# A linear-attention and MLP-mixer kernel: values and kv laid out with 80 columns to a head

## The chip, the cores and the metric

The kernel runs on one core of a Trainium2 chip. The metric is the device time of one execution in microseconds. Three runs of the kernel before took 282.59, 282.40 and 282.09 us, a median of 282.4 us. A profile is one execution with the hardware profiler on; its engines are TensorE (PE in the profile, with PEld for its weight loads), VectorE (DVE), ScalarE (ACT), GpSimd (POOL) and SyncE (SP), which only issues DMAs here.

## The reference

Eight batches of eight heads, 576 positions, 64 numbers to a head. First an attention without softmax:

```python
r = np.maximum(x, 0.0);  phi = concat([r * cos_w, r * sin_w], axis=-1)   # 64 -> 128 features, for q and k
kv  = np.einsum('bhsf,bhsd->bhfd', k_p, v)
z   = np.sum(k_p, axis=2)
num = np.einsum('bhsf,bhfd->bhsd', q_p, kv)
den = np.einsum('bhsf,bhf->bhs', q_p, z)[..., None] + 1e-06
x   = num / den                    # then [batch, 576, 8 heads * 64 = 512]
```

Then an MLP-mixer on x: `u = x + tokens`, where tokens is a two-layer ReLU network along the 576 positions (576 to 256 to 576), and `out = u + channels`, a two-layer ReLU network along the 512 columns (512 to 1536 to 512). Inputs and output are float32; the matmuls are in bf16.

## The kernel before, in words

**Tiling.** A batch's 576 positions are cut into four chunks of 128 positions and a tail of 64. Each of the 128 partitions holds four positions (chunk `ci` is the ci-th position of every partition). The tail's heads 0 to 3 lie in the lower 64 partitions and heads 4 to 7 in the upper 64, so the tail is a fifth chunk with half the heads (`ci == R`, R = 4).

**The front of a batch** (class `Front`) is the attention and the token network. DVE makes the features of k and q in bf16 (`feature`, L193). `values` (L201 on ACT, L203 on DVE) casts v into a tile `v_aug` whose heads are 65 columns apart: 64 values and a column of ones, which was set once ahead of everything (L121) and gives z as the 65th column of kv. There are two such tiles, for even and odd batches. `kv` (L213) multiplies, for each head, the 128 features of a chunk (stationary) with the 65 columns of `v_aug` (moving) and adds up over the chunks in a PSUM tile of two banks, four heads to a bank. `kv_out` (L226 on ACT, in batch 0 one half at L224 on DVE) copies each bank into a bf16 tile, `kv_sb0` and `kv_sb1`, four heads of 65 columns each. `num` (L252, tail L259) multiplies the transposed features of q (stationary, `qpT`) with a head's 65 columns of `kv_sb` (moving) into another two banks. DVE adds 1e-6 to every 65th column (L265), takes the reciprocal (L266) and multiplies the 64 others with it into `x_sb` (L267). `tok1` (L280, L284) and `tok2` (L308, L312) are the token network, L315 adds x. SP transposes u by DMA (L336) into `uT`.

**The back of a batch** (class `Channel`) is the channel network: `c_main` (L418) and `c_tail` (L428) for the twelve tiles of the 1536 hidden columns with a ReLU on ACT (L422, L433), then `o_step` (L444, tail L448), the residual on DVE (L454) and the output DMAs on SP.

**The order** is written out by hand; the tile framework adds only the waits. Batch 0 has its front alone (`first_front`), with filler matmuls of zeros (`busy`, L163) where TensorE would stand idle; `num` puts one such filler into the unused columns of its first PSUM bank (`fill=1`, L247). After that the steps of a batch's `Channel` are interleaved with the pieces of the next batch's `Front` (`pieces`): a table says behind which step each piece is issued, so in the steady batches a chunk of kv or num is eight short matmuls between the long ones of the channel network. The first chunk of num comes one step behind `kv_out`. Each engine takes its instructions in that order.

**Loads.** q, k and v of batch b+2 are loaded by SP while batch b runs (`load_batch`), each tensor by one DMA with runs of 1024 bytes and two with runs of 256 bytes for the tail. In the steady batches SP's queue holds, in this order, five DMA transposes of q's features (L241), the nine loads, outputs, the two transposes of u (L336) and more outputs.

**Tiles in SBUF** lie one behind the other in the order of the pools and of their first use: constants (`v_aug0`, `v_aug1`, then the weights and zeros), then the q, k and v tiles, features, u and `uT`, `qpT`, `kv_sb0`, `kv_sb1`, then `x_sb`, `B1`, `h1T`, `u_bf` and the small ones.

The functions that the change touches, and what calls them:

Of the kernel before, what the change touches and what calls it, by code (L numbers as in the profile page):

```python
# [10 lines left out]
BF16 = mybir.dt.bfloat16  # L11
# [5 lines left out]
def kernel(  # L17
# [15 lines left out]
    nc = tc.nc  # L33

    B, H, S, D = q.shape
# [4 lines left out]
    P = 128  # L40
    R = S // P
    SM = R * P
    ST = S - SM
    NSC = R + 1
# [2 lines left out]
    NCH = D_ch // P  # L47
    HH = H // 2
    D1 = D + 1
    DH = Dm // 2  # L50
    assert S_tok == S and Dm2 == Dm and F == P and 2 * ST == P and H == 2 * HH

# [3 lines left out]
    def half(g):  # L56
        return slice(g * ST, (g + 1) * ST)


    const = ctx.enter_context(tc.tile_pool(name="const", bufs=1))  # L60
# [3 lines left out]
    once = ctx.enter_context(tc.tile_pool(name="once", bufs=1))  # L64
# [52 lines left out]

    v_augs = []
    for i in range(2):
        va = const.tile([P, NSC, H, D1], BF16, name=f"v_aug{i}")  # L120
        nc.vector.memset(va[:, :, :, D:D1], 1.0)  # L121
        v_augs.append(va)

# [37 lines left out]
    def busy(dst, times):  # L161
        for _i in range(times):
            nc.tensor.matmul(dst, ident, zeros[:, 0:dst.shape[-1]], start=True, stop=True)  # L163
# [7 lines left out]
    class Front:  # L171
        def __init__(self, b, res):
            self.qt, self.vt, self.kt = io_tiles[b]
            self.va = v_augs[b % 2]
            self.res = res
            self.kp, self.qp = {}, {}

            self.qpT = once.tile([P, R * H + HH, P], BF16, name="qpT")
            self.kv_sb = [once.tile([P, HH, D1], BF16, name=f"kv_sb{g}") for g in range(2)]
            self.x = once.tile([P, NSC, Dm], BF16, name="x_sb")  # L180

        def feature(self, which, ci, j, heads=(0, H), on_act=False):
# [22 lines left out]
        def kv(self, ci):  # L205
            if ci == 0:
                self.kv_ps = ps_at.tile([P, 2, 512], F32, name="kv_ps", tag="at")
            if ci < R:
                each = [(g, j, slice(0, P), g * HH + j) for g in range(2) for j in range(HH)]
            else:  # L210
                each = [(g, j, half(g), j) for j in range(HH) for g in range(2)]
            for g, j, rows, i in each:
                nc.tensor.matmul(self.kv_ps[:, g, j * D1:(j + 1) * D1],  # L213
                                 self.kp[ci][rows, i, :, :].rearrange("p a b -> p (a b)"),
                                 self.va[rows, ci, i, :],
                                 start=(ci == 0 and j == 0),
                                 stop=(ci == NSC - 1 and j == HH - 1),
                                 skip_group_check=True)

        def kv_out(self, split=False):  # L220
            for g in range(2):
                dst = self.kv_sb[g].rearrange("p j d -> p (j d)")
                if split and g == 1:
                    nc.vector.tensor_copy(dst, self.kv_ps[:, g, 0:HH * D1])  # L224
                else:
                    nc.scalar.copy(dst, self.kv_ps[:, g, 0:HH * D1])  # L226

        def q_trans(self, ci, heads=(0, H)):
            lo, hi = heads if ci < R else (0, HH)
# [14 lines left out]
        def num(self, ci, fill=0):  # L244
            num_ps = ps_at.tile([P, 2, 512], F32, name="num_ps", tag="at")
            if fill:
                busy(num_ps[:, 0, HH * D1:512], 1)  # L247
            den = small.tile([P, 2, HH, 1], F32, name="den")
            if ci < R:
                for h in range(H):  # L250
                    g, j = divmod(h, HH)
                    nc.tensor.matmul(num_ps[:, g, j * D1:(j + 1) * D1],  # L252
                                     self.qpT[:, ci * H + h, :], self.kv_sb[g][:, j, :],
                                     start=True, stop=True)
                n = 2
            else:
                for j in range(HH):
                    for g in range(2):
                        nc.tensor.matmul(num_ps[half(g), 0, j * D1:(j + 1) * D1],  # L259
                                         self.qpT[:, R * H + j, half(g)], self.kv_sb[g][:, j, :],  # L260
                                         start=True, stop=True)
                n = 1
            nv = num_ps[:, 0:n, 0:HH * D1].rearrange("p g (j d) -> p g j d", d=D1)
            den = den[:, 0:n]
            nc.vector.tensor_scalar_add(den, nv[:, :, :, D:D1], 1e-6)  # L265
            nc.vector.reciprocal(den, den)  # L266
            nc.vector.tensor_mul(  # L267
                self.x[:, ci, 0:n * DH].rearrange("p (g j d) -> p g j d", g=n, j=HH),
                nv[:, :, :, 0:D], den.to_broadcast([P, n, HH, D]))

        def tok1(self, mi, chunks):
# [6 lines left out]
            for ci in chunks:  # L278
# [3 lines left out]
                else:  # L282
                    for g in range(2):
                        nc.tensor.matmul(self.b1_ps[mi][:, g * DH:(g + 1) * DH],  # L284
                                         w_tail1[:, g, cols], self.x[:, R, 0:DH],
                                         start=False, stop=False, skip_group_check=True)
# [7 lines left out]
        def tok2(self, ci, pool=None):  # L294
# [8 lines left out]
            else:  # L303
                u_ps = pool.tile([P, Dm], F32, name="u_ps", tag="at")
            n = Dm if ci < R else DH
            for ki in range(NT):
# [4 lines left out]
                for g in range(2):  # L311
                    nc.tensor.matmul(u_ps[half(g), 0:DH], w_tok2[:, ki, SM:S],  # L312
                                     self.B1[:, ki, g * DH:(g + 1) * DH],
                                     start=(ki == 0), stop=(ki == NT - 1))
# [271 lines left out]
```

## Time and profile before

| | |
|---|---|
| median of three runs | 282.4 us |
| the profiled execution | 281.66 us |
| its span | 279.9 us |
| TensorE, DVE, ACT, GpSimd busy | 266.1, 161.1, 123.1, 9.7 us |
| moved by DMA | 52.51 MB |

The busy time of TensorE counts a matmul from its start to its modelled end. Matmuls are pipelined, so one of 65 columns shows about 193 ns while the next one starts some 30 ns behind it; only the starts tell what one costs. In a group's line, the name in front of the arrow is the tile written and those behind it are read; the shape is partitions by elements; the count stands behind an x; then come the group's busy time in us, the mean of one in ns, and the idle time of its engine just ahead of such instructions with what ended it. Lines in order of time begin with the start and the length in us and merge neighbours of one kind, with their count.

### The profile page before, as it was taken

The numbers are of one execution on the slowest core, as the hardware profiler recorded it, in microseconds if no ns is written. First come the engines' busy times: TensorE is split into PE (matmuls) and PEld (weight loads), VectorE is DVE, ScalarE is ACT, GpSimd is POOL, SyncE is SP. The second block draws the span as 40 slices with busy tenths as digits, with TensorE's granted clock in tenths as the row PEclk, the third lists the DMA queues.
The fourth block names the chain that finished last, engine by engine and source line by source line (L and its number), as shares of the span: only waits on it lengthen the run. The fifth ranks groups of instructions, "written<-read, shape, count | busy, mean of one in ns | idle before, by whom it ended". The sixth has DMA issues, their size and how long they took to land.

```text
span 279.9 us, 5799 instructions
## 1 busy us (share of the span) xinstructions
PE 266.1 (95%) x2345; PEld 143.8 (51%) x2370; DVE 161.1 (58%) x395; ACT 123.1 (44%) x237; POOL 9.7 (3%) x20
## 2 busy tenths in 40 slices
PE   5987899999999999999999999999999999999993
PEld 2653666545554455545554455545554455545542
DVE  2877781857576494557566485558467576540021
ACT  2642569048723186036624185137614274225500
POOL 3240020000000000000000000000000000000000
PEclk9999999999999999999999999999999999999999
DMA  6999999921779945992789648994789653161012
GB/s 170 347 192 256 340 181 267 358 89 40 163 215 341 178 112 128 341 294 101 161 257 328 177 103 121 354 267 128 134 260 319 183 96 75 59 160 40 0 75 94
DMA packets 90010, 52.51 MB, mean 188 GB/s; under 512 B 57216, under 2 KB 85760, under 8 KB 89984
## 3 DMA queue, kind: packets, MB, share of 16 engines
q1 hardware_dynamic: 86736, 48.38, 63.1%
q0 software_dynamic: 3248, 3.77, 8.2%
q8 instruction: 18, 0.29, 0.4%
q14 instruction: 8, 0.07, 0.1%
HBM read 35.85 MB, written 9.44 MB: 162 GB/s over the span
## 4 chain that ended last, share of the span: by engine, by line
PE 91%; DVE 3%; ACT 2%; issue 1%; POOL 0%; POOLq 0%; ACTq 0%
PE o_ps L444 29%; PE c_ps L418 29%; PE u_ps L308 5%; PE o_ps L448 5%; PE b_ps L280 4%; PE idle_ps L163 4%; PE ct_ps L428 4%; PE kv_ps L213 4%; PE num_ps L252 3%; PE b_ps L284 1%; ACT qpT L237 1%; DVE x_sb L267 1%; PE qT_ps L235 1%; DVE u_sb L315 1%; PE u_ps L312 1%
## 5 line engine op out<-in xcount | busy, mean ns | idle before, releaser
L444 PE MATMUL o_ps<-w_ch,h1T 128*128 128x512 bf16 x368 | 94.7, 380 | 0.8
L418 PE MATMUL c_ps<-uT,w_ch 128*128 128x512 bf16 (+1 forms) x420 | 95.1, 361 | 0.0
L422 ACT ACTIVATE h1T<-c_ps 128x512 bf16<-128x512 f32 x96 | 57.4, 602 | 62.3 <-PE c_ps L418 62.2
L454 DVE TENSOR_TENSOR o_sb<-o_ps,u_sb 128x512 f32<-128x512 f32 (+1 forms) x40 | 25.5, 637 | 49.4 <-PE o_ps L444 47.7
L444 PEld LDWEIGHTS <-h1T 128*128 128x128 bf16 x384 | 34.5, 98 | 36.3 <-issue 2.6
L418 PEld LDWEIGHTS <-w_ch 128*128 128x128 bf16 x420 | 34.3, 98 | 27.4
L316 ACT CAST u_bf<-u_sb 128x512 bf16<-128x512 f32 (+1 forms) x40 | 22.3, 575 | 21.0 <-DVE u_sb L315 14.5
L428 PEld LDWEIGHTS <-w_ch 128*128 128x128 bf16 x384 | 22.0, 98 | 18.6
L315 DVE TENSOR_TENSOR u_sb<-u_ps,x_sb 128x512 f32<-128x512 f32 (+1 forms) x40 | 25.4, 637 | 9.4 <-PE u_ps L308 7.5
L267 DVE TENSOR_TENSOR x_sb<-num_ps,den 128x512 bf16<-128x512 f32 (+1 forms) x40 | 25.5, 638 | 1.4
L290 ACT ACTIVATE B<-b_ps 128x512 bf16<-128x512 f32 x8 | 4.8, 597 | 47.2 <-PE b_ps L280 47.2
L265 DVE TENSOR_SCALAR den<-num_ps 128x8 f32<-128x8 f32 (+1 forms) x40 | 6.6, 165 | 32.6 <-PE num_ps L252 32.0
L428 PE MATMUL ct_ps<-uT,w_ch 128*128 128x64 bf16 x384 | 24.1, 193 | 0.0
L193 DVE TENSOR_SCALAR qp<-qt,cos_t 128x512 bf16<-128x512 f32 (+1 forms) x44 | 18.8, 431 | 3.0 <-DMA qt<-in_q_dram 3.0
L308 PE MATMUL u_ps<-B,w_tok 128*128 128x512 bf16 x64 | 19.0, 379 | 1.0 <-ACT B L290 0.7
L201 ACT CAST v_aug<-vt 128x512 bf16<-128x512 f32 (+1 forms) x33 | 18.8, 577 | 1.9 <-DMA vt<-in_v_dram 1.9
L193 DVE TENSOR_SCALAR kp<-kt,cos_t 128x512 bf16<-128x512 f32 (+1 forms) x40 | 18.3, 459 | 0.8 <-DMA kt<-in_k_dram 0.8
L280 PE MATMUL b_ps<-x_sb,w_tok 128*128 128x512 bf16 x57 | 16.4, 380 | 1.9 <-DVE x_sb L267 1.8
L193 DVE TENSOR_SCALAR kp<-kt,sin_t 128x512 bf16<-128x512 f32 (+1 forms) x40 | 18.1, 452 | 0.0
L193 DVE TENSOR_SCALAR qp<-qt,sin_t 128x512 bf16<-128x512 f32 (+1 forms) x42 | 18.0, 429 | 0.0
L163 PE MATMUL idle_ps<-zeros,ident 128*128 128x512 bf16 x43 | 12.4, 420 | 3.4 <-DVE zeros L159 3.2
L213 PE MATMUL kv_ps<-v_aug,kp 128*128 128x65 bf16 (+1 forms) x320 | 15.4, 194 | 0.0
(54 smaller groups left out, 173.2 us busy)
## 6 DMA issues: line engine op xcount, KB each, us to landing
kt<-in_k_dram SPq DMA_DIRECT2D x8, 1024.0 KB, 6.7
vt<-in_v_dram SPq DMA_DIRECT2D x8, 1024.0 KB, 7.9
out_dram<-o_sb SPq DMA_DIRECT2D x32, 256.0 KB, 2.5
qt<-in_q_dram SPq DMA_DIRECT2D x7, 1024.0 KB, 7.6
w_ch<-in_moe_w_ch_dram POOLq DMA_DIRECT2D x4, 384.0 KB, 9.4
w_ch<-in_moe_w_ch_dram POOLq DMA_DIRECT2D x3, 512.0 KB, 8.0
qt<-in_q_dram SPq DMA_DIRECT2D x16, 64.0 KB, 6.7
qt<-in_q_dram SPq DMA_DIRECT2D x2, 512.0 KB, 5.0
```

The costliest lines, as they stand in the source:

```text
L163: nc.tensor.matmul(dst, ident, zeros[:, 0:dst.shape[-1]], start=True, stop=True)
L193: nc.vector.tensor_scalar(o_ap, i_ap, scalar1=w, scalar2=0.0, op0=ALU.mult, op1=ALU.max)
L213: nc.tensor.matmul(self.kv_ps[:, g, j * D1:(j + 1) * D1], self.kp[ci][rows, i, :, :].rearrange("p a b -> p (a b)"), self.va[rows, ci, i, : ...
L267: nc.vector.tensor_mul(self.x[:, ci, 0:n * DH].rearrange("p (g j d) -> p g j d", g=n, j=HH), nv[:, :, :, 0:D], den.to_broadcast([P, n, HH, ...
L280: nc.tensor.matmul(self.b1_ps[mi], w_tok1[:, ci, cols], self.x[:, ci, :], start=(ci == 0), stop=(ci == R - 1))
L308: nc.tensor.matmul(u_ps, w_tok2[:, ki, ci * P:(ci + 1) * P], self.B1[:, ki, :], start=(ki == 0), stop=(ki == NT - 1))
L315: nc.vector.tensor_add(res["u"][:, ci, 0:n], u_ps[:, 0:n], self.x[:, ci, 0:n])
L418: nc.tensor.matmul(c_ps[:, lo:hi], w_ch1[:, ki, mi * P:(mi + 1) * P], uT[:, lo // P:hi // P, ki, :], start=(ki == 0), stop=(ki == NCC - 1))
L422: nc.scalar.activation(self.h1T[:, mi, 0:SM], c_ps, AF.Relu)
L428: nc.tensor.matmul(self.ct_ps[:, mi % 6, :], w_ch1[:, ki, mi * P:(mi + 1) * P], self.res["uT"][:, R * NCC + ki % 2, half(ki // 2)], start= ...
L444: nc.tensor.matmul(o_ps, self.h1T[:, ki, ci * P:(ci + 1) * P], w_ch2[:, ki, :], start=start, stop=stop)
L454: nc.vector.tensor_add(o_sb[:, 0:n], o_ps[:, 0:n], res["u"][:, ci, 0:n])
```

## The change

A head's 65 columns stay as they are, but heads lie 80 columns apart in place of 65: in `v_aug` (bf16, from 130 to 160 bytes a head), in `kv_sb` (the same), and in the PSUM tiles of kv and num (fp32, from 260 to 320 bytes a head, four heads to a bank of 2048 bytes). The 15 columns between are never written or read. Matmuls still have 65 moving columns, and there are as many instructions as before. The copies in `kv_out` read and write four runs of 65 columns in place of one run of 260. The filler of `num` fills the columns from 320 to 512 of its bank in place of 260 to 512.

```diff
     D1 = D + 1
+    DP = 80
@@
-        va = const.tile([P, NSC, H, D1], BF16, name=f"v_aug{i}")
+        va = const.tile([P, NSC, H, DP], BF16, name=f"v_aug{i}")
         nc.vector.memset(va[:, :, :, D:D1], 1.0)
@@
-            self.kv_sb = [once.tile([P, HH, D1], BF16, name=f"kv_sb{g}") for g in range(2)]
+            self.kv_sb = [once.tile([P, HH, DP], BF16, name=f"kv_sb{g}") for g in range(2)]
@@ kv
-                nc.tensor.matmul(self.kv_ps[:, g, j * D1:(j + 1) * D1],
+                nc.tensor.matmul(self.kv_ps[:, g, j * DP:j * DP + D1],
                                  self.kp[ci][rows, i, :, :].rearrange("p a b -> p (a b)"),
-                                 self.va[rows, ci, i, :],
+                                 self.va[rows, ci, i, 0:D1],
@@ kv_out
-                dst = self.kv_sb[g].rearrange("p j d -> p (j d)")
+                dst = self.kv_sb[g][:, :, 0:D1]
+                src = self.kv_ps[:, g, 0:HH * DP].rearrange("p (j d) -> p j d", d=DP)[:, :, 0:D1]
                 if split and g == 1:
-                    nc.vector.tensor_copy(dst, self.kv_ps[:, g, 0:HH * D1])
+                    nc.vector.tensor_copy(dst, src)
                 else:
-                    nc.scalar.copy(dst, self.kv_ps[:, g, 0:HH * D1])
+                    nc.scalar.copy(dst, src)
@@ num
-                busy(num_ps[:, 0, HH * D1:512], 1)
+                busy(num_ps[:, 0, HH * DP:512], 1)
@@
-                    nc.tensor.matmul(num_ps[:, g, j * D1:(j + 1) * D1],
-                                     self.qpT[:, ci * H + h, :], self.kv_sb[g][:, j, :],
+                    nc.tensor.matmul(num_ps[:, g, j * DP:j * DP + D1],
+                                     self.qpT[:, ci * H + h, :], self.kv_sb[g][:, j, 0:D1],
                                      start=True, stop=True)
@@ the tail of num, in the same way
-                        nc.tensor.matmul(num_ps[half(g), 0, j * D1:(j + 1) * D1],
-                                         self.qpT[:, R * H + j, half(g)], self.kv_sb[g][:, j, :],
+                        nc.tensor.matmul(num_ps[half(g), 0, j * DP:j * DP + D1],
+                                         self.qpT[:, R * H + j, half(g)], self.kv_sb[g][:, j, 0:D1],
                                          start=True, stop=True)
@@
-            nv = num_ps[:, 0:n, 0:HH * D1].rearrange("p g (j d) -> p g j d", d=D1)
+            nv = num_ps[:, 0:n, 0:HH * DP].rearrange("p g (j d) -> p g j d", d=DP)
```

## The prediction

> **What bounds the kernel now.** I read the page's busy times and slices first, then the chain, then the groups by shape, then the order of instructions inside one batch.
>
> ```profile
> span 279.9 us, 5799 instructions
> PE 266.1 (95%) x2345; PEld 143.8 (51%) x2370; DVE 161.1 (58%) x395; ACT 123.1 (44%) x237; POOL 9.7 (3%) x20
> ...
> PEclk9999999999999999999999999999999999999999
> ...
> PE 91%; DVE 3%; ACT 2%; issue 1%; POOL 0%; POOLq 0%; ACTq 0%
> ```
>
> TensorE is busy 95% of the span at the full granted clock, and 91% of the chain that ended last is its work. From about 48 us on the chain is TensorE almost alone, and the batches repeat every 31.13 us (the first channel matmuls of two batches stand at 189.65 and 220.77 us). So whatever shortens a TensorE instruction there shortens the run; a shorter DVE or ACT instruction does nothing unless TensorE waits for it.
>
> The groups by line and shape (busy us, mean ns of one):
>
> ```profile
> L201 ACT CAST v_aug<-vt 128x512 bf16<-128x512 f32 x26 | 16.1, 624 | 1.9 <-DMA vt<-in_v_dram 1.9
> L252 PE MATMUL num_ps<-kv_sb,qpT 128*128 128x65 bf16 x256 | 14.3, 193 | 0.1
> L213 PE MATMUL kv_ps<-v_aug,kp 128*128 128x65 bf16 x256 | 13.0, 194 | 0.0
> L226 ACT CAST kv_sb<-kv_ps 128x260 bf16<-128x260 f32 x15 | 4.9, 382 | 1.1 <-PE kv_ps L213 1.1
> ```
>
> The change touches 640 TensorE matmuls of 65 columns (256 full and 64 half-array ones for kv, the same for num). A mean of 193 ns is the length of a pipelined one, not what it costs. The cost is the distance from one start to the next, which the order in time shows (start, length, engine, line, count):
>
> ```profile
> 72.43 0.28 PE L428 MATMUL ct_ps<-uT,w_ch 128*128 128x64 bf16 x4
> ...
> 72.54 0.42 PE L213 MATMUL kv_ps<-v_aug,kp 128*128 128x65 bf16 x8
> ...
> 72.80 1.03 PE L418 MATMUL c_ps<-uT,w_ch 128*128 128x512 bf16 x4
> ...
> 75.68 0.65 ACT L226 CAST kv_sb<-kv_ps 128x260 bf16<-128x260 f32 x2
> ...
> 76.10 0.57 PE L252 MATMUL num_ps<-kv_sb,qpT 128*128 128x65 bf16 x8
> ...
> 78.60 0.51 PE L428 MATMUL ct_ps<-uT,w_ch 128*128 128x64 bf16 x12
> ...
> 78.95 0.42 PE L252 MATMUL num_ps<-kv_sb,qpT 128*128 128x65 bf16 x8
> ...
> 79.20 0.38 PE L444 MATMUL o_ps<-w_ch,h1T 128*128 128x512 bf16 x1
> ```
>
> Twelve matmuls of 64 columns take 78.60 to 78.95, 29 ns each. Eight of 65 columns take 72.54 to 72.80 and 78.95 to 79.20, 32 ns each: 3 ns more for one column, where the step from 64 to 512 columns (29 to 216 ns) is 0.42 ns a column. The start stamps of single matmuls say where the 3 ns sit (ns from one start to the next, heads 0 to 7):
>
> ```
> kv,  chunk 0 at  98.97 us: 29 35 33 33 32 33 32 33
> kv,  chunk 1 at 100.21 us: 29 36 32 33 32 34 33 33
> num, chunk 1 at  77.48 us: 29 36 33 31 29 33 32 33
> num, chunk 2 at 110.07 us: 30 35 33 32 30 32 33 32
> ```
>
> In num, heads 0 and 4 are the quick ones: they open the two kv_sb tiles. In kv only head 0 is quick, which opens a v_aug chunk row; head 4 is slow, though its output opens a PSUM bank as head 4 of num does. What the slow ones share is the moving operand's start: 65 bf16 are 130 bytes, so heads i of v_aug start at 130i and those of kv_sb at 130j, past an even boundary by 2 to 14 bytes. The quick ones start at a tile's beginning, or in chunks 1 and 3 of v_aug (1040 bytes a chunk) 16 bytes past a multiple of 32. I read: a 65-column matmul costs 29.4 ns from an aligned start and about 33 from any other.
>
> **The change part by part.**
>
> *Values and kv in SBUF at 80 columns (160 bytes).* All 640 operands then start at multiples of 32 bytes. Sums of eight starts are 260.6 ns for kv in the steady batches and 255.9 for num, against 8 x 29.4 = 235.2. For each of batches 2 to 7:
> - kv, four full chunks: 4 x 25.4 = 0.102 us.
> - num, three full chunks: 3 x 20.7 = 0.062 us. The chunk done first (76.10) stops 0.15 us after four heads for the second of ACT's two kv_sb casts (start to start there is 185 to 186 ns, not 33). Its first half gains nothing; its second half 126 - 117.6 = 0.008 us.
> - the half-array tails, in pairs: 38, 36 and 32 ns between kv's pairs, 52, 36 and 32 between num's. If 32 is the floor, 0 to 0.03 us; I take 0.01, as half of it may be weight loading.
>
> Sum 0.18 us, six times: 1.09. Batch 1: kv 0.10 on the chain (it runs TensorE up to the transposes at 41.58 us, then ACT to 47) and num 0.07. Batch 0: 31 of its kv starts sum to 1002 ns against 911, 0.09, on the chain (kv_ps at 16.15 us for 1.27); then ACT, DVE and the second half of one num, 0.01; its later nums are paced by the DVE multiply (0.69 us a chunk) and give nothing. The last stretch, from 252 us, has no front. All in all 1.36 us. Bounds: 0 if the start is not the cause, 1.6 if the tails and the first num chunk give all they can.
>
> *The casts into kv_sb (L224, L226).* They read four runs of 65 in place of one of 260. The trace has no such read on ACT; ACT's v_aug cast, eight broken runs each way, takes 624 ns against 618 for the flat u_bf cast, so 3 ns for four runs; the farthest row is ACT's permuting copy of w_tok, single-element runs, 638 ns against 602 for h1T's flat 512. By the first 0 to 6 ns for the two, by the second some 40 ns. They end the 0.15 us wait above, so it counts: 6 x 6 ns = 0.04 us, at most 0.25. A gain, a flat 260 having cost more, is not excluded, but is no more than those few ns. Batch 0's DVE cast (429 ns) is on the chain once: DVE's broken read of num_ps takes 691 ns, the flat u_ps read the same, so nothing.
>
> *The reads of num_ps (L265, L267).* Broken runs before and after, only the step grows. Nothing; if they grew, they'd hide behind TensorE in every batch but 0, where five multiplies are on the chain.
>
> *The v_aug casts and memsets.* ACT is busy 13.8 us of a 31.1 us batch, and TensorE waits for no cast. At most 6 ns each comes off, worth nothing. The memsets (92 ns, twice) end before the first q load lets DVE start at 6.18 us.
>
> *The filler matmuls of batch 0* shrink from 252 to 192 columns, 25 ns each, five times; the chain passes them by (it waits for DVE's kv_sb cast or multiplies). Nothing, and the clock is full throughout.
>
> *What moves.* Each v_aug grows from 5200 to 6400 bytes a partition, each kv_sb from 520 to 640. With sizes rounded up to 32 bytes, the tiles behind v_aug shift by 2368 bytes and those behind kv_sb by 2560. They stay aligned to 64 bytes; w_ch2, zeros, uT and the q, k, v tiles go from a multiple of 128 to 64 past one. x_sb and B, moving operands too, stand 64 past one already, and their 512-column matmuls (L280, L308) keep the same 216 ns as L418 and L444. So TensorE loses nothing. For DMA destinations, all at multiples of 256 bytes before, the trace has no row; this is the third case below.
>
> Sum: -1.36 + 0.04 = -1.3 us. The profiled execution took 281.66 us (279.9 of span and 1.8 around it), 0.74 under the median of 282.4. 281.66 - 1.3 = 280.4 on its scale, **281.1 us** on the median's. A difference of about 0.2% (0.56 us) is what a measurement of this kernel can tell from no change.
>
> **The rivals.**
>
> *The start is not what costs.* Then 65 columns stay at 32.5 ns and the time at 282.4. For it: in kv the quick first head is followed by one of 35 or 36, so that pair averages the rest. Against it: head 4 of num, mid-run, is quick with a normal one behind it, and the start is all that sets it apart from kv's head 4. The Trainium skill, "SBUF — State Buffer", section "Door 1: The DMA port swizzle", says that SBUF has 16-byte lines and that each access that crosses into a new one pays. By that rule alone nothing changes: 130 bytes touch nine lines from an aligned start and nine from one that is 2 to 14 bytes off. The rows speak against it, since quick and slow heads touch the same number.
>
> *DMA into the shifted tiles gets slower* (the other side). The loads of batch b+2 run from 201.5 to 217.2 us, 15.7 us, and the two uT transposes queue behind them on SP. Their landing stamps leave little before the next batch's first channel matmul, which needs uT:
>
> ```
> second uT landed  95.58 126.23 157.34 189.16 220.43 250.67
> first c_ps        96.27 127.39 158.52 189.65 220.77 251.90
> room, us           0.69   1.16   1.18   0.49   0.34   1.23
> ```
>
> With loads in front of five of them, a delay d costs the sum of what exceeds each room. 0.93 us (6% of 15.7) eats the whole 1.3 us; 1.12 us (7%) makes the run 0.56 us slower. For it: the DMA engines are 77 to 84% busy in these batches. Against it: loads read HBM in runs of 1024 bytes, unchanged, and only the SBUF end moves. From there three or four batches stall for each further us: at 1.12 us the time is 283.0, at 10% (1.57 us) the stalls sum to 3.7 us and the time is 284.8. The Trainium skill, "DMA: Bandwidth & Descriptors", section "How a descriptor splits into AXI transactions", has a transaction start at 256-byte boundaries, bytes before the start costing beats; were writes charged as it says of fetches, a 1024-byte run 64 bytes past one would take 34 beats for 32 and a 256-byte run 10 for 8. By it, with a ninth of the bytes in short runs, the loads take an estimated 8% longer (1.26 us) and the run 283.5 us. No run so far shows it.
>
> *ACT takes the gain back.* A broken PSUM read on ACT that cost 100 ns each would lengthen the wait in the first num chunk by 0.2 us in six batches, 1.2 us: no change, 282.3. Nothing in the ACT rows comes near it.
>
> **How the numbers follow.** Start alignment works and shows: 0.74, time 280.7 to 281.7, likeliest 281.1. No gain: 0.11, 282.1 to 282.7. DMA slower: 0.09, a third within 0.2%, the rest above, from 283.0 on. ACT: 0.02, no change. Something unseen: 0.04, mostly slower. Faster 0.75, same 0.16, slower 0.09. The range reaches up to take in most of no gain: 280.4 to 282.6.
>
> **What would show it.** Right: starts in kv and num 29 to 30 ns apart for every head; busy time of L213 and L252 down by some 0.8 us and 0.6 us; batch period 31.13 to about 30.95 us; the first num chunk still with its 0.15 us stop; L226 within 10 ns of 382. Wrong: starts still 32 to 33 ns apart (first rival); starts at 29 with the period not shorter, and TensorE waiting for uT ahead of L418, loads landing later than 15.7 us after their issue (second); the stop at the first num chunk longer and L226 near 480 ns (third).

## The result and the profile after

The changed kernel takes 283.48 us (median of 20 runs), the kernel before beside it 282.52 us: a ratio of 1.0041, 95% interval 1.0024 to 1.0058. It is 1.2 us (0.7 to 1.6) slower where 1.3 us faster was forecast, and the time lies outside the range given. The profiled execution took 284.99 us, one of the longer ones, so its trace shows where time goes, but more of it than usual.

What was forecast of the matmuls did come. The order in time of the kernel after, in a steady batch (start, length, engine, line, count):

```profile
70.38 0.28 PE L430 MATMUL ct_ps<-uT,w_ch 128*128 128x64 bf16 x4
70.49 0.41 PE L214 MATMUL kv_ps<-v_aug,kp 128*128 128x65 bf16 x8
70.74 1.02 PE L420 MATMUL c_ps<-uT,w_ch 128*128 128x512 bf16 x4
```

Eight kv matmuls stand at 70.49 to 70.74 us. By the start stamps eight of them take 245.9 ns in the mean (260.7 before) and eight of num 245.1 (255.7). A batch without a stop takes 31.04 us, before 31.13.

The loss is elsewhere. The page of the kernel after: span, busy time, SP's DMA queue (packets, MB, share of 16 engines' time) and the chain by engine.

```profile
span 283.2 us, 5799 instructions
...
PE 266.1 (94%) x2345; PEld 142.9 (50%) x2370; DVE 161.3 (57%) x395; ACT 123.0 (43%) x237; POOL 11.3 (4%) x20
...
q1 hardware_dynamic: 86736, 48.38, 67.8%
...
PE 77%; DMA 15%; POOL 2%; SPq 2%; issue 1%; DVE 1%; ACT 0%; POOLq 0%
```

The same queue before:

```profile
q1 hardware_dynamic: 86736, 48.38, 63.1%
```

The same packets and megabytes took 63.1% of 16 engines' time before and take 67.8% now, and DMA, which had no part in the chain, holds 15% of it. Who waited for whom, after (us in total, times, longest):

```profile
ACT v_aug L202 <- DMA vt<-in_v_dram: 4.1, 1, 4.1
...
PE kv_ps L214 <- ACT v_aug L202: 1.6, 1, 1.6
...
PEld L420 <- DMA uT<-u_bf: 1.2, 1, 1.2
...
PE o_ps L446 <- DMA w_ch<-in_moe_w_ch_dram: 0.9, 1, 0.9
```

ACT's wait for v was 1.9 us before; the other three waits are new. The order in time in batch 0, before:

```profile
14.95 1.45 ACT L201 CAST v_aug<-vt 128x512 bf16<-128x512 f32 x3 [1.88 <-DMA vt<-in_v_dram]
...
15.98 1.43 PE L213 MATMUL kv_ps<-v_aug,kp 128*128 128x65 bf16 x40
```

and after:

```profile
17.12 1.45 ACT L202 CAST v_aug<-vt 128x512 bf16<-128x512 f32 x3 [4.06 <-DMA vt<-in_v_dram]
...
17.79 0.98 PE L214 MATMUL kv_ps<-v_aug,kp 128*128 128x65 bf16 x26 [1.57 <-ACT v_aug L202]
```

The first large v load landed at 17.09 us, before at 14.92. The fillers no longer cover that, and kv begins at 17.79 us instead of 15.98. The wait for the weights w_ch, which ends at 50.97 us, adds 0.9 us. By the first channel matmul of the second batch the run is 2.6 us late (67.79 against 65.15 us), and the later batches lose 0.7 more in sum: they win 0.09 us each, but the one at 161.80 us starts 0.05 us behind the landing of uT and 0.9 us late, the one at 224.21 us 0.14 us behind it and 0.3 us late. The loads of the five steady batches with loads take 16.0 us in the mean from first issue to last landing, before 15.2.

The stretch from 8 to 15 us, in which the DMA engines have little but loads to do, shows it in one line. Windows of the kernel before (length, busy us and count of PE, PEld, DVE, ACT, POOL, granted clock, busy share of the DMA engines, GB/s):

```profile
8.00:15.00 7.00, 6.95 (x60) 4.29 (x60) 6.15 (x20) 4.56 (x10) 2.88 (x4) 1.00 1.11 341
```

and of the kernel after:

```profile
8.00:15.00 7.00, 6.95 (x60) 4.19 (x60) 5.52 (x19) 4.50 (x9) 1.59 (x3) 1.00 1.10 303
```

By these two executions the DMA engines are as busy and move 11% less.

### The profile page after: what moved, and what is told of

It reads as the page before. It is cut to its first block, busy times and chain, and to the rows that moved or that the text cites. A ratio compares the mean times of both kernels' runs of the same rounds, so it can differ in the third digit from the quotient of the medians.

```text
span 283.2 us, 5799 instructions
## 1 busy us (share of the span) xinstructions
PE 266.1 (94%) x2345; PEld 142.9 (50%) x2370; DVE 161.3 (57%) x395; ACT 123.0 (43%) x237; POOL 11.3 (4%) x20
## 3 DMA queue, kind: packets, MB, share of 16 engines
q1 hardware_dynamic: 86736, 48.38, 67.8%
## 4 chain that ended last, share of the span: by engine, by line
PE 77%; DMA 15%; POOL 2%; SPq 2%; issue 1%; DVE 1%; ACT 0%; POOLq 0%
PE o_ps L446 27%; PE c_ps L420 26%; DMA w_ch<-in_moe_w_ch_dram 7%; PE o_ps L450 4%; PE u_ps L310 4%; PE b_ps L282 4%; DMA vt<-in_v_dram 4%; PE ct_ps L430 3%; DMA kt<-in_k_dram 3%; PE num_ps L254 3%; PE kv_ps L214 3%; DMA uT<-u_bf 2%; SPq L82 1%; POOL w_ch L150 1%; PE b_ps L286 1%
## 5 line engine op out<-in xcount | busy, mean ns | idle before, releaser
L318 ACT CAST u_bf<-u_sb 128x512 bf16<-128x512 f32 (+1 forms) x40 | 22.3, 575 | 21.1 <-DVE u_sb L317 16.6
L317 DVE TENSOR_TENSOR u_sb<-u_ps,x_sb 128x512 f32<-128x512 f32 (+1 forms) x40 | 25.4, 637 | 9.4 <-PE u_ps L310 7.5
L214 PE MATMUL kv_ps<-v_aug,kp 128*128 128x65 bf16 (+1 forms) x320 | 14.9, 193 | 1.6 <-ACT v_aug L202 1.6
```

The costliest lines, as they stand in the source:

```text
L214: nc.tensor.matmul(self.kv_ps[:, g, j * DP:j * DP + D1], self.kp[ci][rows, i, :, :].rearrange("p a b -> p (a b)"), self.va[rows, ci, i, 0:D1],
L317: nc.vector.tensor_add(res["u"][:, ci, 0:n], u_ps[:, 0:n], self.x[:, ci, 0:n])
L318: nc.scalar.copy(self.ub[:, ci, 0:n], res["u"][:, ci, 0:n])
```

## The experiments

Two theories stood against each other. Theory 1: DMA into tiles that start off a multiple of 256 bytes is slow; the wider v_aug tiles moved everything behind them by 2368 bytes, so q, k, v, the weights, uT and qpT went from a multiple to 64 past one. Theory 2: something in the 80-column layout itself, its strides or its broken casts, disturbs the loads. The two medians of a row were taken on the same chip.

| what lies where | us | before | ratio (95%) | first v landed, us |
|---|---|---|---|---|
| 80 columns, the change | 283.48 | 282.52 | 1.0041 (1.0024 to 1.0058) | 17.09 |
| 80 columns, other tiles as before | 281.70 | 282.94 | 0.9967 (0.9947 to 0.9987) | 15.55 |
| 65 columns, all tiles 64 off | 285.00 | 282.94 | 1.0072 (1.0050 to 1.0093) | 17.23 |
| 65 columns, q, k, v 64 off | 284.27 | 282.94 | 1.0056 (1.0033 to 1.0078) | 17.13 |
| 65 columns, transposes' tiles 64 off | 282.84 | 282.94 | 0.9992 (0.9977 to 1.0007) | 15.48 |
| 65 columns, q, k, v 32 off | 284.89 | 282.64 | 1.0088 (1.0069 to 1.0106) | 17.53 |
| 65 columns, q, k, v 192 off | 283.84 | 282.64 | 1.0048 (1.0033 to 1.0063) | 16.92 |
| 96 columns, other tiles as before | 281.71 | 282.64 | 0.9975 (0.9962 to 0.9987) | 15.80 |
| 80 columns, outputs and u aligned too | 281.78 | 282.64 | 0.9971 (0.9954 to 0.9988) | 14.63 |

**The layout without the shift.**

```diff
             v_augs.append(va)
+    pad_v = const.tile([P, 96], BF16, name="pad_v")
+    nc.vector.memset(pad_v[:, 0:1], 0.0)
@@
-            self.kv_sb = [once.tile([P, HH, DP], BF16, name=f"kv_sb{g}") for g in range(2)]
+            self.kv_sb = [once.tile([P, HH * DP + 32 * g], BF16, name=f"kv_sb{g}")[:, 0:HH * DP]
+                          .rearrange("p (j d) -> p j d", d=DP) for g in range(2)]
```

> The 80-column layout as in the change, with 192 bytes left free behind the two v_aug tiles and 64 behind kv_sb1, so that every other tile lies at the same distance from a multiple of 256 bytes as in the kernel before. Theory 1 (the loss comes from DMA into tiles that start 64 bytes past a multiple of 256): first v load landed near 14.9 us as before (17.1 after the change), steady loads 15.2 us from issue to last landing, TensorE's stops for v_aug and uT gone, starts of eight kv matmuls still 246 ns in sum, so batches of 31.04 us and a time of about 281.8 us, 0.7 under before. Theory 2 (the 80-column layout itself disturbs the loads, by its strides in SBUF or the broken casts): loads as late as after the change and about 283.5 us.

Measured: 0.9 us under the kernel before (0.4 to 1.5). Its page, span, SP's queue and the chain:

```profile
span 279.8 us, 5825 instructions
...
q1 hardware_dynamic: 86736, 48.38, 62.4%
...
PE 92%; DVE 3%; ACT 2%; issue 1%; POOL 0%; POOLq 0%; ACTq 0%
```

The steady loads take 14.8 us, the stops of kv and of the channel matmuls for uT are gone, and batches take 31.04 us (one of them 31.12). The first large v load landed at 15.55 us, later than the 14.9 expected, but in the runs with the loads at multiples of 256 bytes it lies anywhere from 14.63 to 15.80, and in those with the loads off from 16.92 to 17.53. Theory 2 falls: the layout is the same, and the loads are among the early ones again. DMA is out of the chain too, which says less: one execution with 72 columns and every tile as before (below) has 13% of DMA in its chain, and a stop of 0.9 us for w_ch as in the changed kernel, so that stop is not the shift's alone.

**The shift without the layout.**

```diff
             v_augs.append(va)
+    pad_v = const.tile([P, 32], BF16, name="pad_v")
+    nc.vector.memset(pad_v[:, 0:1], 0.0)
@@
-            self.kv_sb = [once.tile([P, HH, D1], BF16, name=f"kv_sb{g}") for g in range(2)]
+            self.kv_sb = [once.tile([P, HH * D1 + 96 * g], BF16, name=f"kv_sb{g}")[:, 0:HH * D1]
+                          .rearrange("p (j d) -> p j d", d=D1) for g in range(2)]
```

> The kernel before with its 65 columns; only 64 bytes are left free behind v_aug (and 192 behind kv_sb1), so that weights, q, k, v, features, uT and qpT start 64 bytes past a multiple of 256, as the change put them. Theory 1: loads 5% longer in the steady batches, first v load landed near 17.1 us, and about 284.2 us (0.96 us that the change lost and 0.7 that its matmuls gained). Theory 2: as before, 282.5 us.

Measured: 2.0 us slower (1.4 to 2.6), a little more than the 1.7 expected. Its windows:

```profile
8.00:15.00 7.00, 7.00 (x61) 4.18 (x59) 5.60 (x20) 4.51 (x9) 1.47 (x2) 1.00 1.12 297
```

The loss of the change is all here, without the change. The two runs also add up: 2.0 us lost by the shift and 0.9 won by the layout make 1.1 us, and the change measured 1.2.

**Which transfers.** The q, k and v tiles alone, by 64 bytes left free behind the constants and 192 behind the three tiles:

```diff
     io = ctx.enter_context(tc.tile_pool(name="io", bufs=2))
+    gap = ctx.enter_context(tc.tile_pool(name="gap", bufs=1))
     phi = ctx.enter_context(tc.tile_pool(name="phi", bufs=NSC))
@@
     nc.vector.memset(zeros, 0.0)
+    pad_io = gap.tile([P, 96], BF16, name="pad_io")
+    nc.vector.memset(pad_io[:, 0:1], 0.0)
+    pad_c = const.tile([P, 32], BF16, name="pad_c")
+    nc.vector.memset(pad_c[:, 0:1], 0.0)
```

> The kernel before with the q, k and v tiles alone moved 64 bytes past a multiple of 256; weights, features and the targets of the DMA transposes stay. Theory 1 with the loads as the cause: nearly all of the loss of the run with everything moved, 283.5 to 284.2 us, first v load near 17 us. Theory 1 with the transposes (targets and sources) as the cause: 282.5 us and the first loads as before.

and everything behind those tiles in their place (the 64 bytes stand in the pool between, the 192 behind kv_sb1):

> The kernel before with the q, k, v and weight tiles in their places and only what lies behind them moved by 64 bytes: features, u, uT, qpT and kv_sb, so the DMA transposes of q read and write, and those of u write, 64 bytes past a multiple of 256. Theory 1 with the loads as the cause: 282.5 to 282.8 us, transposes of q at 2.8 us from issue to landing. With the transposes as the cause: 283.5 us or more, transposes of q at 3.2 us or more, uT landing close ahead of the next batch's first channel matmul.

The loads alone cost 1.6 us (0.9 to 2.2); the first v landed at 17.13 us and steady loads took 16.1 us. With the transposes' tiles moved the time stayed, although they do get slower. The DMA view of that run (kind, count, median us from issue to landing):

```profile
qpT<-qp SPq DMA_TRANSPOSE x30, 3.2
uT<-u_bf SPq DMA_TRANSPOSE x12, 4.2
```

Before, and with the loads alone moved, the q transposes take 2.8 us. In the steady batches of that run each lands 1.3 us or more ahead of its num, so 0.4 us more is hidden. What is left between 1.6 and 2.0 us for the weights' tiles is within the intervals.

**How far off.** The same edit with 32 and with 192 bytes ahead of q, k and v:

> The kernel before with the q, k and v tiles alone 32 bytes past a multiple of 256 (64 in the run before this one: 284.3 us, first v load landed at 17.13 us, before 14.92). If a row that starts off the boundary costs one more transaction, however far off it is, the same as at 64 bytes: about 284.3 us and a first v load near 17.1 us. If it pays for the bytes ahead of its start (one more 32-byte beat in place of two), half of it: 283.4 us and 16.0 us.

> As above with the q, k and v tiles 192 bytes past a multiple of 256. One more transaction: about 284.3 us, first v load near 17.1 us, as at 64 bytes. Paying for the bytes ahead of the start (six beats in place of two): three times the lateness, first v load near 21.5 us and a time above 289 us, since the steady loads would take over 18 us where 15 to 16 fit.

Windows of the run with 64 bytes (the q, k and v tiles alone):

```profile
8.00:15.00 7.00, 7.00 (x60) 4.05 (x58) 5.57 (x19) 4.51 (x9) 1.62 (x3) 1.00 1.12 301
```

with 32 bytes:

```profile
8.00:15.00 7.00, 7.00 (x61) 4.29 (x60) 5.45 (x20) 4.50 (x9) 1.47 (x2) 1.00 1.11 289
```

and with 192:

```profile
8.00:15.00 7.00, 7.00 (x59) 4.13 (x58) 5.98 (x21) 4.50 (x9) 1.85 (x3) 1.00 1.12 295
```

289, 301 and 295 GB/s at 32, 64 and 192 bytes, against 341 in the kernel before and 319 to 347 in all runs with the loads at multiples of 256: there is a price for being off, and it doesn't grow with the distance. Paying for the bytes ahead of the start, which should have put the first v load at 21.5 us for 192 bytes, falls: it landed at 16.92. At 32 bytes the median is the worst of the three, above that at 192 with separate intervals; why, no run tells.

The account of one more transaction a run fits this and is not shown by it. The packet records of the traces speak against one fixed sum on every run. From 2 to 18 us, 3072 packets of 1024 bytes bring all of the first batch but its tails. With the loads at multiples of 256 at least three quarters of them take 46 ns (means of 48 to 50). With the loads off, 30 to 38% still take 46 ns, and the others mostly take from 47 to 100 ns (means of 57 to 60, at all three distances). Packets of 256 bytes keep their median of 18 ns, with means of 18 and of 19 to 20. What makes some packets slow stays open.

The section of the Trainium skill that the prediction named ("DMA: Bandwidth & Descriptors", "How a descriptor splits into AXI transactions") has transactions start at 256-byte boundaries, and bytes ahead of the start, which it calls fetched, cost beats. These writes into SBUF show no such cost of the bytes ahead. That a start off the boundary costs something agrees with it, but no run lies 128 bytes past a multiple of 256, so these runs can't tell a boundary of 256 bytes from one of 128.

**Wider rows.** `DP = 96`, free bytes as in the first experiment:

> 96 columns to a head in place of 80 (192 bytes in SBUF, 384 in PSUM), with every other tile at the distance from a multiple of 256 bytes that it had before, as in the 80-column run with free bytes (281.7 us). With 80 columns two of eight starts are 35 to 36 ns and not 29, and heads alternate between 0 and 32 bytes past a multiple of 64. If that half line is what costs, 96 columns show 29 to 30 ns for all eight, sums near 235 in place of 246 ns, and some 0.5 us less, 281.2 us. If it comes from 65 columns themselves or from weight loads, the sums stay at 246 ns and the time at 281.7 us.

Sums of eight starts stayed at 245.9 and 246.1 ns, and the time at 281.7 us. So the slow starts that remain don't come from heads that start 32 bytes past a multiple of 64.

**PSUM alone, and 72 columns.** One execution each: `DP` only in the PSUM tiles; and `DP = 72` with free bytes as above.

> 80 columns to a head in the PSUM tiles alone; v_aug and kv_sb keep 65, and no tile in SBUF moves. If the start in SBUF is what a matmul of 65 columns pays for: starts as in the kernel before, sums of eight near 260 ns in kv and 256 in num, the v_aug and kv_sb tiles' first heads alone quick. If the odd start in PSUM were it: 246 ns. The cast into kv_sb on ACT, now reading four broken runs, shows what that read costs by itself (382 ns before).

> 72 columns to a head (144 bytes in SBUF, so heads start at multiples of 16 and every other one off a multiple of 32), with every other tile at its old distance from a multiple of 256 bytes. If a start at a multiple of 16 bytes is enough: sums of eight at 246 ns as with 80 columns. If it takes 32: every other head of 33 ns, sums near 253 ns.

The order in time with PSUM alone at 80 columns:

```profile
69.28 0.42 PE L214 MATMUL kv_ps<-v_aug,kp 128*128 128x65 bf16 x8
69.55 1.02 PE L420 MATMUL c_ps<-uT,w_ch 128*128 128x512 bf16 x4
```

and with 72 columns:

```profile
69.30 0.41 PE L217 MATMUL kv_ps<-v_aug,kp 128*128 128x65 bf16 x8
69.55 1.03 PE L423 MATMUL c_ps<-uT,w_ch 128*128 128x512 bf16 x4
```

By the stamps the sums of eight are 260.2 and 257.3 ns (kv, num) with PSUM alone, as before the change, and 245.8 and 245.3 ns with 72 columns. So the start in PSUM alone is worth nothing, and with heads at multiples of 16 bytes in SBUF the gain is there. A multiple of 8 is not enough: in the kernel before, head 4 of a v_aug chunk lies 520 bytes from its start, 8 past a multiple of 16, and its start costs 33 ns. Whether the gain in SBUF comes with the PSUM tiles still at 65 columns, no run tells. That size of a line, 16 bytes, is what the Trainium skill gives ("SBUF — State Buffer", "Door 1: The DMA port swizzle"). But a count of touched lines, nine from every start, wouldn't tell the two apart. The times, 281.97 and 282.58 us against one run of 283.06 us before, are single runs that decide nothing.

**A better version.** The first experiment with x, B, h1T, u in bf16 and the output tiles at multiples of 256 bytes too:

```diff
-            den = small.tile([P, 2, HH, 1], F32, name="den")
+            den = small.tile([P, 4, HH, 1], F32, name="den")[:, 0:2]
@@
-            self.kv_sb = [once.tile([P, HH * DP + 32 * g], BF16, name=f"kv_sb{g}")[:, 0:HH * DP]
+            self.kv_sb = [once.tile([P, HH * DP + 128 * g], BF16, name=f"kv_sb{g}")[:, 0:HH * DP]
```

> The 80-column layout with free bytes, and in addition x, B, h1T, u in bf16 and the output tiles moved from 64 or 192 bytes past a multiple of 256 to a multiple, so that the output DMAs and the transposes of u read from one too. If reads by DMA pay for the distance as the loads' writes do, outputs take less than 2.6 us and transposes of u less than 3.8 us from issue to landing, with more room ahead of the next batch, and 281.4 us or a little less. If only writes pay, 281.7 us.

281.78 us, ratio 0.9971 (0.9954 to 0.9988): no better than 0.9967. Outputs took 2.4 us and transposes of u 3.8 us from issue to landing, the same as in the first experiment. No price shows for reads off the boundary. Both versions beat the kernel before by 0.8 or 0.9 us, and so the changed one; the simpler is the first.

## Why the prediction was wrong

**The likeliest case failed at its chance, not its mechanism.** A matmul of 65 columns does cost less from an aligned start, PSUM's start by itself gives nothing, and the clock, the casts, the reads of num_ps and the fillers did as forecast: the ACT cast takes 389 ns against 382, inside the 10 ns allowed. The stop ahead of the first num chunk stayed too.

**The step that failed** is the weighing of the second rival. It named the cause, the shift of 2368 bytes that takes every DMA destination off a multiple of 256, and said that the trace had no row for it. Then it set this case at 0.09 on the argument that loads read HBM in unchanged runs of 1024 bytes "and only the SBUF end moves". In the sum the shift stands as nothing; alone, without the layout, it cost 2.0 us (1.4 to 2.6). The windows from 8 to 15 us, with the DMA engines at 1.1 before the change and after it, show that no spare time hid the SBUF end: what a run costs more there comes straight out of the rate. An argument from the other end of the transfer took the place of the missing row.

**Its price was read at one place only.** It was worked out from the 0.34 to 1.23 us of room ahead of the steady batches. In sum that part was about right: with loads 0.9 us longer two batches stopped, for 0.9 and 0.3 us, and by those rooms 0.9 us of delay would have cost 1.2 us. That they agree is in part luck: the larger stop came in a batch with 1.18 us of room, whose loads took 16.6 us in place of 14.0. But batch 0 was left out of it. There the first loads run back to back, the first v load lands 2.2 us later, and the fillers end 1.6 us ahead of kv; in the profiled execution most of the loss is there before the second batch begins. The rival's 283.5 us, worked out from beats, is within 0.1 us of what was measured, and that is luck: the loads became 0.9 us longer and not 1.26, the price doesn't follow the beats, batch 0 was missing from it and the gain was taken for twice its size. Its sum at 10% is also off: 1.57 us exceeds the five rooms by 4.0 us in all, not 3.7, which would have made 285.1 us.

**The gain was mis-sized.** The sum took 29.4 ns for an aligned matmul, from single quick heads. All eight aligned take 245.9 ns in kv, 30.7 each, since the second and the seventh are still 36 and 35 ns. The first rival had seen that a quick head is followed by one of 35 or 36, and the sum let that go. With 14.8 ns a chunk in kv in place of 25.4, and 10.6 in num in place of 20.7, a batch wins 0.09 us and not 0.18, as the batch period says (31.13 to 31.04 us). The busy time of the full kv and num matmuls fell by 0.4 and 0.3 us, half of the 0.8 and 0.6 named as signs. Eight batches make 0.7 us in place of 1.36; the three versions without the shift measured 0.7 to 0.9.

**The other rivals.** The first, that the start is not what costs, fell; so did the third, that ACT takes the gain back.

## What to carry to other kernels

A tile that grows moves all that is allocated behind it, and what it does to a matmul may be the smaller half: work out the new start of every DMA destination, and keep it at a multiple of 256 bytes with a few free bytes, where the DMA engines are busy. When the trace has no row for something that a change does to the busiest queue, its absence is no ground for a small chance; a bound belongs there, at each place where that queue is waited for. A single quick instruction within a run is not the rate of a run of them.

## What had not been expected of the hardware

- With the loads' rows in SBUF 32, 64 or 192 bytes past a multiple of 256, the stretch from 8 to 15 us ran at 289 to 303 GB/s (DMA engines at 1.10 to 1.12), and from a multiple at 319 to 347 (1.01 to 1.12), with runs of 1024 and 256 bytes. Off a multiple, most packets of 1024 bytes took more than 46 ns; from one, most took 46.
- DMA transposes of q with tiles 64 bytes off take 3.2 us from issue to landing, against 2.8.
- Matmuls of 65 columns from aligned starts go 29 or 30 ns apart, with one in four of 34 to 37, at 72, 80 and 96 columns alike; those of 64 columns keep 28 to 30 ns in runs of twelve. Where the slow ones come from stays open.
- ACT's cast of 260 numbers takes 6 or 7 ns more when its output is broken into four runs (389 and 388 ns), and nothing more when only its PSUM input is (382 ns).
